# RWKV-6 attention and an MLP mixer on one core: the first batch's states, weight writes, loads and hand-written order

## The chip, the cores and the metric

The kernel runs on one core of a Trainium2 chip. The time is the device time of one launch in microseconds: 509.42 us is the median of three runs (509.24 to 509.84). One further execution was profiled; every duration below comes from that execution, whose span is 509.5 us.

## The reference

```python
B, H, S, D = 4, 8, 768, 48
state = zeros((B, H, D, D))
for t in range(S):                                   # attention, w lies in 0.8 to 0.95
    cur = einsum('bhd,bhe->bhde', u[None] * kt, vt)
    y[:, :, t] = einsum('bhd,bhde->bhe', rt, state + cur)
    state = wt[:, :, :, None] * state + einsum('bhd,bhe->bhde', kt, vt)
x = y.transpose(0, 2, 1, 3).reshape(B, S, H * D)     # 4 x 768 x 384
xt = x.transpose(0, 2, 1)                            # then the mixer
h = maximum(xt @ w_tok1, 0) @ w_tok2                 # 768 -> 256 -> 768 over tokens
u = x + h.transpose(0, 2, 1)
out = u + maximum(u @ w_ch1, 0) @ w_ch2              # 384 -> 1536 -> 384 over channels
```

The four mixer weights arrive as float64. The kernel loads their bits as pairs of 32-bit words and makes float32 of them on the chip.

## The kernel before, in words

**Units.** The attention of one batch is cut into three units of 256 tokens; `unit(i)` (from L352) makes the functions of unit i, called e0, e1, e2 for the first batch. A unit holds four chunks of 64 tokens (c = 0, 1 by j = 0, 1). Its steps, in order of need, are:
- `own_u` (ScalarE, four instructions, L278) multiplies the keys by u; `own_gram` (TensorE, L262) makes the products of a token with itself; `own_put` (VectorE, L400) masks them into `at`.
- `ends` (VectorE scan, L377) and `begins` (scan, L385) make the running products of w from both sides; `keys` (L382) and `queries` (L388) multiply k and r by them. `ranges` (ScalarE, L369) counts values outside a safe range; its result is read only near the end of the kernel.
- `tokens` (TensorE, eight transposes, L292) and `copied` (ScalarE, L293) turn the keys; `carry` (TensorE, `outer`, L308) makes each chunk's own part of the state, all four in one PSUM tile `kv_ps` that exists once.
- For each chunk, `scaled` (ScalarE, four instructions, L443, called t) multiplies the state by the chunk's whole decay into `before`, and `updates` (VectorE, L451 and L453, called s) adds the chunk's part from `kv_ps` into a new `state` in SBUF. This is a chain: t needs the s of the chunk in front of it, and s needs t.
- `gram` (L262) and `mask` (VectorE, L274) make the products of tokens within a chunk; `before()` (`across`, TensorE, L322), `seen` (ScalarE, L331) and `after` (`within`, TensorE, L343) form the output in PSUM, and `taken` (ScalarE, L349, three copies) moves it to `x`.

The grams and the outputs share two PSUM tiles (`ps_g`): each takes the tile that the second one before it gave back through its own_put, mask or taken.

**Weights.** `convert` (L202) works on a pair of blocks of 512 values per partition: `load` (two DMAs, L211), `exponent` (x, VectorE, L214), `raise_two` (p, ScalarE, L217), `mantissa` (m, VectorE, L220), `signs` (g, ScalarE, L223), `add` (VectorE, L226) and `put` (VectorE: one bf16 multiplication, L229, then one write for each block, L232). Three pairs hold w_tok1 and w_tok2 (`to_tok`, numbers 0 to 2), nine hold w_ch1 and w_ch2 (`to_ch`; its pair 0 is number 3 in the order below). The raw words lie in buffers, `bits64`; a load waits until the pair that used its buffer before is done.

**The prologue.** The first batch's three units, the `to_tok` conversions and the first mixer product `hidden` (h[2c + i], c a block of 128 tokens, i one of two halves, L747, two TensorE instructions each) stand in one order written out by hand: the call of `strict(...)` at the end of the planner's section. Each engine (TensorE, VectorE, ScalarE, and SP, which issues the DMAs) takes its own instructions in the order of that list. The relu of `hidden` (L749) closes the prologue, and `back` (L754) is the first TensorE work behind it. Loads called ahead of `strict` are issued first, in the order of the text: w0, rk0 (k then r), w1, v0, rk1, to_tok 0, rk2, v1, to_tok 1.

**After the prologue.** The mixer of batch b is interleaved with the attention of batch b + 1 by `interleaved`, a planner in the kernel that merges lists of pieces by due times (its costs are constants in the text). For the first batch these lists are the mixer, units 3 to 5, and `early_forms`: the `to_ch` conversions, three of the `ranges` (e1's second and e2's two; e1's first stands last in the hand-written list), and forms of the weights for the later batches. `back`, then the transposes to `xT` (L762, copied by ScalarE, L763) and `up` (L772) follow each other there.

**Buffers.** `ws` holds two buffers of w: units 0 and 2 share `ws[0]`, so w2 is loaded after unit 0's queries. `xpool` rotates two buffers of x; the first batch takes one of them.

## Time and profile before

| what | value |
| --- | --- |
| median of three runs | 509.42 us |
| span of the profiled execution | 509.5 us |
| mean granted TensorE clock | 0.981 of full |
| TensorE (PE) busy | 479.2 us, 94% of the span |
| weight loads of TensorE (PEld) busy | 404.4 us |
| VectorE (DVE) busy | 382.2 us |
| ScalarE (ACT) busy | 266.9 us |
| chain that ended last | PE 82%, DVE 8%, DMA 3%, ACT 3% |

Busy is the time in which an engine had an instruction in execution. A row of the timeline gives the start, the length, the engine, the line, the operation, the output and inputs, how many instructions are merged, and in brackets how long the engine stood idle ahead of it and what ended that wait. "issue" there means that the engine waited for nothing the profile shows. SPq is the queue of SP, from which nearly all DMAs are issued. The granted clock is the share of TensorE's full clock that the throttle let through.

### The profile page before, as it was taken

How to read it: one execution, taken by the hardware profiler on the slowest of the kernel's cores; microseconds unless marked ns; L12 is line 12 of the kernel's file. 1: busy time of each engine (PE TensorE's matmuls, PEld its weight loads, DVE VectorE, ACT ScalarE, POOL GpSimd, SP SyncE). 2: the span in 40 equal slices, each digit the busy share in tenths (PEclk: the TensorE clock that was granted, in tenths of full speed). 3: DMA queues.
4: the chain of work that ended last, by engine and by line, in shares of the span. 5: the costliest groups of instructions: out<-in, count | busy, mean ns of one | idle time of the engine just before them, and what ended most of it. 6: DMA issues, size and time to landing. Idle time of an engine off the chain costs nothing.

```text
span 509.5 us, 12748 instructions
## 1 busy us (share of the span) xinstructions
PE 479.2 (94%) x5218; PEld 404.4 (79%) x5218; DVE 382.2 (75%) x588; ACT 266.9 (52%) x631; POOL 53.2 (10%) x58
## 2 busy tenths in 40 slices
PE   3489999999999999999999999999999999999995
PEld 3477578866687667998989957999989958999995
DVE  7997998997764588787986948787985906566562
ACT  3876977755554544456545234556555324253350
POOL 0000000000000000311302000302212101130230
PEclk9769999999999999999999999999999999999999
DMA  8842937774560673583846571473725441345231
GB/s 305 321 177 64 302 115 257 243 220 136 158 196 26 192 216 116 177 233 99 262 122 210 187 249 60 140 227 97 258 70 156 143 153 48 98 135 171 78 111 50
DMA packets 48975, 83.76 MB, mean 164 GB/s; under 512 B 4816, under 2 KB 40272, under 8 KB 48912
## 3 DMA queue, kind: packets, MB, share of 16 engines
q1 hardware_dynamic: 48768, 82.90, 51.6%
q8 instruction: 42, 0.69, 0.6%
q14 instruction: 21, 0.17, 0.1%
q10 hardware_dynamic: 144, 0.00, 0.0%
HBM read 71.87 MB, written 11.01 MB: 163 GB/s over the span
## 4 chain that ended last, share of the span: by engine, by line
PE 82%; DVE 8%; DMA 3%; ACT 3%; issue 2%; SPq 0%; DVEq 0%; ACTq 0%
PE h_ps L783 9%; PE z_ps L772 9%; PE joint_ps L612 8%; PE ends_ps L641 7%; PE ends_ps L643 7%; PE o_ps L655 7%; PE o_ps L657 7%; PE o_ps L656 6%; PE h_ps L593 4%; PE h_ps L586 3%; PE gram L262 3%; PE kv_ps L308 3%; PE y_ps L343 2%; PE y_ps L322 2%; PE h_ps L747 2%
## 5 line engine op out<-in xcount | busy, mean ns | idle before, releaser
L634 POOL TENSOR_TENSOR z_high<-z_high 128x384 fp32r<-128x384 f32 x48 | 52.0, 1086 | 441.2 <-ACT z_high L619 237.6
L613 ACT ACTIVATE mid<-joint_ps 128x384 f32<-128x384 f32 x72 | 34.9, 485 | 64.5 <-PE joint_ps L612 63.3
L626 DVE TENSOR_TENSOR ends_ps<-ends_ps,mid 128x384 f32<-128x384 f32 x72 | 40.6, 563 | 32.4 <-PE ends_ps L643 19.8
L612 PE MATMUL joint_ps<-z_more,forms 128*128 128x384 f32 x216 | 51.6, 347 | 0.8 <-DVE z_more L564 0.8
L655 PE MATMUL o_ps<-forms,z_high 128*128 128x384 f32 x144 | 49.7, 345 | 1.7 <-DVE x L664 1.7
L641 PE MATMUL ends_ps<-x_forms,forms 128*128 128x384 f32 x216 | 49.5, 337 | 0.8 <-DVE z_high L630 0.8
L772 PE MATMUL z_ps<-xT,wch 128*128 128x256 f32 x216 | 49.4, 383 | 0.8 <-ACT xT L763 0.8
L643 PE MATMUL ends_ps<-x_forms,ring 128*128 128x384 f32 x216 | 49.3, 337 | 0.0
L657 PE MATMUL o_ps<-forms,z_high 128*128 128x384 f32 x144 | 48.8, 339 | 0.2
L783 PE MATMUL h_ps<-wch,z 128*128 128x384 f32 x144 | 48.5, 490 | 0.0
L656 PE MATMUL o_ps<-ring,z_high 128*128 128x384 f32 x144 | 48.5, 336 | 0.0
L443 ACT ACTIVATE before<-state,to_end 112x48 f32<-112x48 f32 x148 | 37.3, 326 | 19.1 <-DVE state L453 19.0
L772 PEld LDWEIGHTS z_ps<-xT,wch 128*128 128x128 f32 x216 | 40.1, 190 | 6.6 <-ACT xT L763 1.0
L783 PEld LDWEIGHTS h_ps<-wch,z 128*128 128x128 f32 x144 | 26.8, 190 | 17.1
L612 PEld LDWEIGHTS joint_ps<-z_more,forms 128*128 128x128 f32 x216 | 38.3, 188 | 2.4 <-DVE z_more L564 1.1
L664 DVE SCALAR_TENSOR_TENSOR x<-o_ps,x 128x384 f32<-128x384 f32 x36 | 19.8, 549 | 27.0 <-PE o_ps L656 26.8
L641 PEld LDWEIGHTS ends_ps<-x_forms,forms 128*128 128x128 f32 x216 | 38.6, 188 | 1.5 <-DVE z_high L630 1.5
L643 PEld LDWEIGHTS ends_ps<-x_forms,ring 128*128 128x128 f32 x216 | 38.5, 188 | 0.0
L655 PEld LDWEIGHTS o_ps<-forms,z_high 128*128 128x128 f32 x144 | 27.0, 188 | 2.9 <-DVE x L664 2.5
L657 PEld LDWEIGHTS o_ps<-forms,z_high 128*128 128x128 f32 x144 | 27.0, 188 | 1.5 <-DVE x L665 1.5
L622 ACT ACTIVATE z_high<-z_high 128x384 fp32r<-128x384 f32 x48 | 25.3, 526 | 4.1
L656 PEld LDWEIGHTS o_ps<-ring,z_high 128*128 128x128 f32 x144 | 27.1, 188 | 0.0
(153 smaller groups left out, 931.1 us busy)
## 6 DMA issues: line engine op xcount, KB each, us to landing
ring<-third SPq DMA_DIRECT2D x144, 192.0 KB, 3.6
raw<-in_w_ch_dram SPq DMA_DIRECT2D x16, 512.0 KB, 4.9
rk<-in_rk_dram SPq DMA_DIRECT2D x36, 192.0 KB, 5.5
near<-in_near_dram SPq DMA_DIRECT2D x8, 768.0 KB, 4.7
w<-in_w_dram SPq DMA_DIRECT2D x10, 520.5 KB, 3.7
vt<-in_v_dram SPq DMA_DIRECT2D x12, 384.0 KB, 3.5
out_dram<-x SPq DMA_DIRECT2D x18, 192.0 KB, 3.0
raw<-in_w_tok_dram SPq DMA_DIRECT2D x6, 512.0 KB, 9.5
```

The costliest lines, as they stand in the source:

```text
L443: act.mul(t[:ROWS, a], state[bt, g][:ROWS, a], by_last(c, j)[:, a:a + 1])
L612: pe.matmul(b, joint[m], xf[2][:, m], start=m == 0, stop=m == 2)
L613: act.mul(mid(jt), b, BASE / (BASE - 1.0))
L626: dve.tensor_add(a, a, mid(jt))
L634: pool.tensor_add(z_form(jt, 2), z_form(jt, 2).bitcast(f32), z_form(jt, 1).bitcast(f32))
L641: pe.matmul(a, up[m], xf[0][:, m], start=m == 0, stop=False)
L643: pe.matmul(a, low[:, m], xf[1][:, m], start=False, stop=m == 2)
L655: pe.matmul(a, z[0], up, start=first, stop=False, skip_group_check=True)
L656: pe.matmul(a, z[1], held[bt, s, half, 1, jt], start=False, stop=last, skip_group_check=True)
L657: pe.matmul(b, z[2], joint, start=first, stop=last, skip_group_check=True)
L772: pe.matmul(ps, now["wch1"][:, m, ts(jt, 128)], xT[:, m, ts(s, SEG)], start=(m == 0), stop=(m == DM // 128 - 1))
L783: pe.matmul(ps, zs[s][:, jt, ts(n, 128)], now["wch2"][:, jt, :], start=(jt == 0), stop=(jt == NJ - 1))
```

## The change

It has seven parts, all in the first batch or in the conversions:
- **States by TensorE.** For batch 0, `updates` makes no VectorE instruction any more. `outer` sets `start` only for the first product of each quarter and bank of `kv_ps`; `updates` multiplies `before` by the identity on TensorE (112 x 128 by 112 x 192, float32) and lets it accumulate onto the chunk's part in `kv_ps`. `scaled` then reads the state from PSUM.
- **Wider writes.** Where the two blocks of a pair lie so that one access pattern covers both, `put` writes them with one instruction of 1024 values; for pairs side by side the load lays the raw words out to match.
- **Constants.** Four copies and casts (L173, L174, L179) go from VectorE to ScalarE.
- **Places.** w2 gets the second x buffer, free in the first batch; `to_tok` 2 gets the buffer of `xT`, and each `to_tok` pair now has raw words of its own.
- **Loads first.** w2, rk2, all three `to_tok` pairs and `to_ch` 0 are issued ahead of the hand-written list.
- **Order.** The hand-written list is another one. It also holds the three `ranges` that were in the planner's list, and the relu is a step of its own, `rectified`.
- The planner's piece `ends` of unit 3 waits for one of the `ranges` no more.

```diff
@@ -123,8 +123,11 @@
 
+    second_x = xpool.tile([128, C, DM], f32, name="x")
+    ws.append(second_x.rearrange("p c e -> p (c e)")[:, :WCOLS])
+
     def w_of(i):
-        return ws[i % 2 if i <= UB else 1]
+        return ws[i if i < UB else 1]
 
@@ -170,13 +173,13 @@
     for j in range(2):
-        dve.tensor_copy(on_diagonal[ts(j, T)], ident[ts(j, T), ts(j, T)])
-    dve.tensor_copy(diagonal, on_diagonal)
+        act.copy(on_diagonal[ts(j, T)], ident[ts(j, T), ts(j, T)])
+    act.copy(diagonal, on_diagonal)
     pool.memset(strictly, 1.0)
...
                            pattern=[[1, T]], channel_multiplier=-1)
-    dve.tensor_copy(before_it, strictly)
+    act.copy(before_it, strictly)
 
@@ -206,9 +209,25 @@
 
+        (a, _), (b, _) = pair
+        c, k = a.shape[1:]
+        (row, _), (one, _) = a.ap[1:]
+        apart = b.offset - a.offset if a.tensor is b.tensor else None
+        beside = apart == k * one
+        if beside:
+            whole = bass.AP(a.tensor, a.offset, [list(a.ap[0]), [row, c], [one, 2 * k]])
+        elif apart is not None and (c == 1 or apart == c * row):
+            whole = bass.AP(a.tensor, a.offset, [list(a.ap[0]), [apart // c, 2 * c], [one, k]])
+        else:
+            whole = None
+
         def load():
             for n, (dst, src) in enumerate(pair):
-                sp.dma_start(d64[:, ts(n, 2 * PIECE)].rearrange("p (c k) -> p c k", c=dst.shape[1]), src)
+                if beside:
+                    to = d64.rearrange("p (c n k) -> p n c k", n=2, c=c)[:, n]
+                else:
+                    to = d64[:, ts(n, 2 * PIECE)].rearrange("p (c k) -> p c k", c=dst.shape[1])
+                sp.dma_start(to, src)
 
@@ -227,8 +246,8 @@
             dve.tensor_mul(factor, factor, sign)
-            for n, (dst, src) in enumerate(pair):
-                x, by = (t[:, ts(n, PIECE)].rearrange("p (c k) -> p c k", c=dst.shape[1]) for t in (mf, factor))
+            for dst, cols in [(whole, slice(0, 2 * PIECE))] if whole is not None else [(dst, ts(n, PIECE)) for n, (dst, _) in enumerate(pair)]:
+                x, by = (t[:, cols].rearrange("p (c k) -> p c k", c=dst.shape[1]) for t in (mf, factor))
                 dve.scalar_tensor_tensor(dst, x, 2.0 ** -20, by, op0=ALU.mult, op1=ALU.mult)
@@ -301,12 +320,14 @@
         kv = ps_a.tile([128, 2, 512], f32, name="kv_ps", tag="a")
+        begun = set()
         for c in range(UC):
...
                         pe.matmul(kv[ts(q, P), j, ds((c * A + a) * D, D)], kT[ts(j, T), c, a, ts(q, P)],
-                                  vt[ts(j, T), c, ts(2 * a + q, D)], start=True, stop=True)
+                                  vt[ts(j, T), c, ts(2 * a + q, D)], start=(q, j) not in begun, stop=True, skip_group_check=True)
+                        begun.add((q, j))
         return kv
@@ -444,7 +465,12 @@
             g = 2 * (half * UC + c) + j
-            if g < 2 * C - 1:
+            if g < 2 * C - 1 and bt == 0:
+                state[bt, g + 1] = L["kv"][:ROWS, j, ds(c * A * D, A * D)].rearrange("p (a e) -> p a e", a=A)
+                if g:
+                    pe.matmul(L["kv"][:, j, ds(c * A * D, A * D)], ident[:ROWS], L["before"][g][:ROWS].rearrange("p a e -> p (a e)"),
+                              start=False, stop=True, skip_group_check=True)
+            elif g < 2 * C - 1:
                 new = state[bt, g + 1] = apool.tile([128, A, D], f32, name="state", bufs=3)
@@ -745,8 +771,9 @@
             pe.matmul(sums[i], now["wtok1"][:, c, ts(i, 128)], x_of()[:, c, :], start=(c == 0), stop=(c == C - 1))
-            if c == C - 1:
-                act.activation(h1[:, i, :], sums.pop(i), AF.Relu)
+
+        def rectified(i):
+            act.activation(h1[:, i, :], sums.pop(i), AF.Relu)
 
@@ -787,7 +814,7 @@
 
-        return dict(hidden=hidden, back=back, turn=turn, up=up, down=down)
+        return dict(hidden=hidden, rectified=rectified, xT=xT, back=back, turn=turn, up=up, down=down)
 
@@ -811,7 +838,7 @@
         loads = piece(lambda: load_rk(i + 1), "loads")
-        ends = piece(e["ends"], "ends", ("DVE", 2.6, last("small", "large", "by3") + ((("of", 0),) if i == UB else ())))
+        ends = piece(e["ends"], "ends", ("DVE", 2.6, last("small", "large", "by3")))
         keys = piece(e["keys"], "keys", ("DVE", 1.25, k("ends")))
@@ -927,29 +954,35 @@
     h = [lambda i=i, c=c: turned["hidden"](i, c) for c in range(C) for i in range(DTOK // 128)]
-    to_tok = conversion((wtok1, w_tok1, 2, 256), (wtok2, w_tok2, 2, 256), rooms=lambda n: (n % 2, n % 2))
+    rectified = [lambda i=i: turned["rectified"](i) for i in range(DTOK // 128)]
+    bits64.append(turned["xT"].rearrange("p m t -> p (m t)").bitcast(u32)[:, :4 * PIECE])
+    to_tok = conversion((wtok1, w_tok1, 2, 256), (wtok2, w_tok2, 2, 256), rooms=lambda n: (3, 0) if n == 2 else (n, n))
     to_ch = conversion((now["wch1"], w_ch1, 1, 512), (now["wch2"], w_ch2, 4, 128), rooms=lambda n: (n % 2, 0, rks[2][:, ts(n % 2, PIECE)].bitcast(bf16)) if n else (2, 1))
+    load_w(2)
+    load_rk(2)
     to_tok[0][0]()
-    load_rk(2)
     load_v(1)
-    to_tok[1][0]()
+    for steps in (*to_tok[1:], to_ch[0]):
+        steps[0]()
 
     e0, e1, e2 = (unit(i) for i in range(UB))
-    (_, x0, m0, p0, add0, g0, put0), (_, x1, m1, p1, add1, g1, put1), (load2, x2, m2, p2, add2, g2, put2) = to_tok
-    load3, x3, m3, p3, add3, g3, _ = to_ch[0]
+    (_, x0, m0, p0, add0, g0, put0), (_, x1, m1, p1, add1, g1, put1), (_, x2, m2, p2, add2, g2, put2) = to_tok
+    _, x3, m3, p3, add3, g3, _ = to_ch[0]
     in_turn.update({pe.engine: None, dve.engine: None, act.engine: None, sp.engine: None})
     s0, s1, s2 = (e["updates"] for e in (e0, e1, e2))
     t0, t1, t2 = (e["scaled"] for e in (e0, e1, e2))
-    strict(*e0["own_u"], e0["ends"], e0["own_gram"], e0["begins"], e0["keys"], e0["tokens"], *e0["copied"], e0["queries"], lambda: load_w(2),
-           e0["gram"], *e1["own_u"], e1["ends"], e0["carry"], *e0["ranges"], e0["own_put"], e0["mask"], e1["own_gram"], s0[0], t0[1],
-           x0, p0, s0[1], t0[2], m0, g0, e1["begins"], s0[2], t0[3], add0, s0[3], t1[0], e0["before"], e0["seen"], put0, load2,
-           e1["keys"], e0["after"], *e2["own_u"], e1["tokens"], *e1["copied"], e1["queries"], e1["own_put"], e1["carry"], *e0["taken"],
-           lambda: load_v(2), e1["gram"], e2["ends"], g1, s1[0], t1[1], e2["keys"], e2["tokens"], s1[1], t1[2], e2["own_gram"], *e2["copied"],
-           e2["begins"], s1[2], t1[3], e1["mask"], load3, s1[3], t2[0], *h[:2], e2["carry"], e1["before"], h[2], e2["queries"], s2[0], t2[1],
-           e2["own_put"], e1["seen"], s2[1], t2[2], e2["gram"], x1, p1, e1["after"], m1, s2[2], t2[3], e2["mask"], h[3], add1,
-           e1["taken"][0], put1, to_ch[1][0], lambda: (load_w(3), load_rk(3), load_v(UB)), e2["before"], e2["seen"], *e1["taken"][1:],
-           x2, s2[3], e2["after"], *h[4:8], *e2["taken"], m2, p2, x3, add2, g2, m3, h[8], h[10], h[9], h[11], p3, put2, add3, g3,
-           to_ch[2][0], e1["ranges"][0])
+    strict(e0["ends"], e0["own_u"][0], e0["own_u"][1], e0["own_u"][2], e0["own_u"][3], e0["begins"], e0["own_gram"], e0["ranges"][0],
+           e0["ranges"][1], e1["own_u"][0], e0["keys"], e1["own_u"][1], e1["ends"], e0["queries"], e1["own_u"][2], e0["tokens"], e0["copied"][1],
+           e0["copied"][0], e1["own_u"][3], e0["own_put"], e1["ranges"][0], e1["begins"], e0["carry"], s0[0], e1["own_gram"], e1["keys"], t0[1],
+           s0[1], t0[2], e2["own_u"][0], e1["queries"], e2["own_u"][1], e0["gram"], e1["own_put"], x0, s0[2], e1["tokens"], t0[3], s0[3],
+           e2["own_u"][2], e1["copied"][0], t1[0], e1["copied"][1], lambda: load_w(3), p0, e0["before"], e0["mask"], e1["carry"], e0["seen"], g0,
+           e0["after"], s1[0], e2["own_u"][3], e0["taken"][0], t1[1], e2["own_gram"], e2["ends"], e0["taken"][1], s1[1], t1[2], m0, e0["taken"][2],
+           e2["keys"], e2["tokens"], lambda: load_rk(3), lambda: load_v(2), s1[2], e1["gram"], add0, x1, e2["copied"][0], t1[3], s1[3],
+           e2["own_put"], e2["copied"][1], to_ch[2][0], t2[0], e1["before"], put0, e2["carry"], e1["mask"], e2["ranges"][0], h[1], e1["seen"], s2[0],
+           e1["after"], e2["begins"], p1, m1, t2[1], g1, s2[1], e2["queries"], t2[2], h[0], add1, e2["gram"], e1["taken"][0], s2[2], h[2], x2,
+           e1["taken"][1], lambda: load_v(UB), e2["mask"], to_ch[1][0], t2[3], e1["taken"][2], m2, h[3], put1, e2["before"], p2, h[4], e2["seen"],
+           e2["after"], h[5], g2, h[6], add2, m3, h[7], g3, x3, e2["taken"][0], e2["taken"][1], e2["taken"][2], add3, h[8], h[9], p3,
+           e1["ranges"][1], put2, h[10], h[11], rectified[0], rectified[1], e2["ranges"][1])
 
@@ -1016,10 +1049,9 @@
         stored = [(("kept", i), lambda i=i: sp.dma_start(kept[i], (wtok1, wtok2)[i].rearrange("p c k -> p (c k)")), ()) for i in range(2)]
-        ranges = [(("of", n), f, (("ACT", 1.4, ()),)) for n, f in enumerate((e1["ranges"][1], *e2["ranges"]))]
         formed = [e for n in range(HALF) for e in splits(0, n)]
         late = [e for n in range(HALF) for e in splits(1, n)]
-        return first[:1] + each[1] + ranges + sum(each[2:], []) + stored + formed + late[:1] + late[5:6] + late[1:5] + late[6:-5 * AFTER], late[-5 * AFTER:]
+        return first[:1] + each[1] + sum(each[2:], []) + stored + formed + late[:1] + late[5:6] + late[1:5] + late[6:-5 * AFTER], late[-5 * AFTER:]
 
@@ -1115,6 +1147,7 @@
                 plain["hidden"](i, c)
+            plain["rectified"](i)
         for c in range(C):
```

## The prediction

> **What bounds the kernel now.** I first read the busy time of each engine by stretches (columns: stretch and length, then PE, PEld, DVE, ACT, POOL, granted clock, DMA share, GB/s).
>
> ```profile
> 0.00:54.00 54.00, 36.41 (x977) 28.77 (x977) 47.31 (x66) 34.91 (x89) 1.26 (x10) 0.84 0.63 224
> 54.00:70.00 16.00, 14.61 (x63) 9.81 (x64) 14.90 (x23) 15.20 (x26) 0.00 (x0) 1.00 0.82 237
> 70.00:100.00 30.00, 30.00 (x361) 25.86 (x360) 27.50 (x39) 21.94 (x49) 0.00 (x0) 1.00 0.64 204
> 100.00:140.00 40.00, 40.00 (x436) 25.71 (x435) 33.80 (x43) 22.70 (x47) 0.00 (x0) 1.00 0.58 180
> ```
>
> From 70 us on TensorE never stops, so whatever is saved there on another engine is worth nothing. In the first 54 us VectorE is the fullest engine and TensorE has 17.6 us of idle time, with a mean clock of 0.84. The change is worth what it does to the moment at which `back` (L754) starts, plus the 1.4 us that TensorE idles in 54 to 70. So I read the timelines of the first 56 us next, VectorE first, then TensorE, then SP.
>
> ```profile
> 16.93 0.34 DVE L451 COPY state<-kv_ps 112x192 f32<-112x192 f32 x1
> 18.35 0.35 DVE L453 TENSOR_TENSOR state<-before,kv_ps 112x192 f32<-112x192 f32 x1 [0.48 <-ACT before L443]
> 40.63 0.35 DVE L453 TENSOR_TENSOR state<-before,kv_ps 112x192 f32<-112x192 f32 x1 [2.70 <-PE kv_ps L308]
> 43.97 1.31 DVE L274 COPY_PREDICATED at<-before_it,gram 128x1024 f32<-128x1024 uint8 x1
> ```
>
> VectorE runs from 3.81 (first scan) nearly without a break; its two named stops stand at state updates, one behind e2's `carry`. The mask at 43.97 is e2's, the last VectorE work that e2's `after` needs.
>
> ```profile
> 18.39 0.85 PE L262 MATMUL gram<-rk,near 48*64 48x64 f32 x42 [1.94 <-issue]
> 32.68 1.58 PE L292 MATMUL k_ps<-ident,first 128*128 128x128 f32 x8 [1.73 <-issue]
> 36.11 2.93 PE L747 MATMUL h_ps<-x,wtok 128*128 128x384 f32 x4
> 46.91 1.15 PE L343 MATMUL y_ps<-vt,at 64*64 64x48 f32 x64 [0.27 <-ACT seen L331]
> 47.99 5.43 PE L747 MATMUL h_ps<-x,wtok 128*128 128x384 f32 x16
> 54.00 4.14 PE L754 MATMUL h_ps<-h,wtok 128*128 128x384 f32 x12 [0.58 <-ACT h L749]
> ```
>
> The end of the prologue is a tail: mask until 45.28, `after` until 48.06, eight `hidden` until 53.42, relu, `back` at 54.00: 8.7 us from the mask. Two stalls of 1.94 and 1.73 us are marked "issue". `hidden` costs 2.93/4 = 0.73 us an instruction at 36 us and 5.43/16 = 0.34 at 48 us: the granted clock is 0.50 to 0.53 in the stretches 20 to 30 and 35 to 40.
>
> **The change part by part.**
>
> *VectorE up to e2's mask.* I use the distance from one start to the next in an unbroken row, about 0.09 us under the printed length: scan with memset and reciprocal 2.55 (2.80 for e0's), begins 2.25, keys and queries 1.13, own_put 1.12, mask 1.20, exponent and mantissa 0.60, add 1.13, put 0.72 + 1.21. The new list puts these ahead of e2's mask or ends with it: three ends 7.90, three begins 6.75, six keys and queries 6.78, three own_put 3.36, three masks 3.60, x0, m0, x1, m1, x2 3.00, two adds 2.26, put0 1.86 (0.72 and one wide write; the nearest row of 128x1024 float32 from SBUF, L226, is 1.22 long against 1.29 for two halves, so 0.07 less). Sum 35.5; 3.81 + 35.5 = 39.3. The same count for the old list adds 11 updates at 0.26 (2.9), the four constants (10.02 to 10.64, 0.62) and 0.07, and lacks add1 and x2 (1.73), which it had behind the mask: 37.4, to 41.2. The mask really left VectorE at 45.2, so 4.0 us were waits: 2.70, 0.48 and small ones. By VectorE alone the mask comes 5.9 us earlier, if no wait is left.
>
> *The order's tail.* From mask to `back` the new order has `after`, seven `hidden` (h5 to h11; the last four behind `taken`) and the relus: three `taken` 1.45 and the last four `hidden` 2.7, with `after` 1.2, `before`'s rest 1.3 and the relu 0.6, plus 0.6 in which ScalarE still finishes g3 ahead of `taken` and 0.7 of hand-overs. That is 8.6, the same. ScalarE has p3 (1.14) and e1's second ranges (1.34) between `taken` and the relu, 2.5 beside 2.7 of `hidden`: just hidden; a late p3 would delay the relu by as much. put2 is the last VectorE work: 39.3 + m2 0.60, put1 1.93, add2 1.13, m3 and x3 1.20, add3 1.13, put2 1.86 = 47.2, and `back` needs it only from its third block, 2.7 us in.
>
> *States on TensorE.* An add has no row. Its two passes over 192 columns are bounded below by 2 x 0.12 (L292, 128 columns, x8 in 0.97 at full clock) and above by 2 x 0.34 (L747, 384 columns); by columns 0.34, with some 0.16 to drain. Ten of them: 3.4 us of TensorE, 2.4 to 6.8. As a link of the chain an add takes about 0.5 where the VectorE add took 0.35; a link is then 0.5 + 1.01 (L443, four instructions) + two hand-overs of 0.07, 1.65 against 1.5. Eleven links are 18 us, spread over some 24, so the chain binds only where TensorE is late. TensorE takes its list in order: while an add waits for ScalarE, the next gram or transposes behind it wait too, and their mask or copy. e1's `carry` now also waits until t of e1's first chunk has read `kv_ps`.
>
> *TensorE's own sum* up to e2's `after`: per unit own_gram 1.08, tokens 0.95, carry 1.05, gram 1.08, before 1.1, after 1.1 = 6.4, three times 19.1; adds 3.4; five `hidden` 3.4: 25.9 us at full clock, from 8.4 on (rk0 lands at 8.1 at the latest) to 42.4: 34.0, so 8.1 of slack. The two first steps ran at half clock in the old trace too (1.98 and 1.94): 1.9. If the "issue" stalls come again: 3.7. A small product at half clock takes about 1.7 times as long (1.96 against 1.15 for L343), so a cold microsecond loses 0.41. With both charges 2.5 us are left, enough for 6 us of cold clock; before it was 17 us.
>
> *The clock.* In the old trace it fell at about 19.5, after a stretch with 1.6 us of work in 3.4, and at 33.1, after one with 1.7, and came back at 29.7 and 40. The new list keeps TensorE at 25.9/34 = 76% of the time, against 21.8/39.7 = 55%, so I expect less cold time, some 7 us. [...]
>
> *Placed one by one.* I put each instruction at the later of its engine's previous one and its inputs. The old list, with the old cold stretches, so gives e2's `after` at 48.2 (48.06 in the trace) and `back` at 54.2 (54.00). The new one gives 48.5 warm without stalls, 50.3 warm with both stalls, 50.3 with 10 cold microseconds without, 51.7 with 7 cold and both stalls. I take **50.3**, 3.7 us earlier.
>
> *Loads.* SP has eight DMAs in flight (v1 was issued at 9.38, when w1 landed). At the old rate, 390 to 404 GB/s from 10 to 20 us, the new sequence lands w2 at 14, rk2 at 16.6, to_tok 0 at 19.3 (was 15.3; needed at 20.4), v1 at 20.2, to_tok 1 and 2 at 22.9 and 25.6, to_ch 0 at 28.2, and behind w3 and rk3 v2 at 32.6, where e2's `carry` wants it at 31.7 to 34: at most 0.9 us, counted in the placing. In the old list SP stood from 13.4 to 23 for put0's buffer.
>
> *The mixer after 54.* ScalarE sheds three or four ranges of 1.34 between 55.9 and 65.5, where it is at 15.2 of 16 and TensorE waits for `xT` copies; of the 1.4 us idle there, 0.6 is the relu. I take 0.4 of the remaining 0.8, bounds 0 and 0.8. The constants on ScalarE (under 1 us) lie in its 3.9 us wait for rk0. The other wide puts, seven at 0.07, and `ends` freed from its ranges lie beside a saturated TensorE: 0.
>
> Sum: 3.7 + 0.4 = 4.1 off the span of 509.5, 505.4; the median of the runs shown stands 0.1 below that span: **505.3 us**.
>
> **The rivals.**
> - *VectorE's sum decides.* TensorE keeps up, warm and without stalls: `back` at 48.5, 5.5 earlier, and 0.8 in the mixer: 503.2 on the span, 503.1 on the median. For it: 76% use. Against it: the stalls lay where DMA was busy, and the new list keeps it full until 32.
> - *TensorE becomes the bound* and it gets slower: with both stalls and ten or more cold microseconds behind the start, its adds, taken in order, pass each delay on to the next gram and its mask. Ten cold ones place `back` at 54.5, the old 17 at 56.2: 0.5 to 2.2 later, 509.9 to 511.6. It decides from 9 cold microseconds on with both stalls. For it: the first steps start cold and e0's gram no longer follows straight on the transposes. Against it: fuller stretches.
> - *Given back in the mixer.* `interleaved` gets other lists and so another merge; VectorE is at 92% from 70 to 100, and where its conversions came late for `up`, TensorE would wait what it gained. VectorE's list ends 6 us earlier too, which speaks against it. A loss of 3.7 gives 509.0.
>
> **How the numbers follow.** Forecast 0.50, VectorE's sum 0.27, given back 0.10, TensorE bound 0.13. The range runs from 502.6 (48.5, all of the mixer's idle, 0.5 for adds at their lower bound) to 509.4 (`back` level with before), leaving out some 0.05 below and 0.12 above. A difference of 0.2% (1.0 us) is what can be told from no change here: faster than 508.4 has 0.80, within 0.10, slower than 510.4 0.10.
>
> **What would show it.** `back`'s first row at 50.3, e2's mask at 41 to 43; no L451 or L453 on VectorE before `back`; ten more TensorE rows of 112x192 in the state's line; the 2.70 stop gone; fewer than 10 cold microseconds; v2 landing by 33; TensorE idle under 1 us in the 16 us behind `back`. I am wrong if TensorE's rows wait on ScalarE's `before` for more than 6 us in all, if the clock stays at 0.5 past 30, or if `back` comes early and the end does not follow.

## The result and the profile after

The changed kernel takes 516.57 us (median of four executions, 514.80 to 516.58) against 509.36 before: a ratio of 1.0126, 95% interval 1.0106 to 1.0146. It is slower, outside the predicted range. The ratios below leave out one slow execution, of `al_warm_vec` (689.24 us at a mean clock of 0.653).

The profiled execution has a span of 513.1 us against 509.5, so 3.6 us of the loss are in the traces. The other half is not: in every execution the time is 1.7 us above the span, but the traced execution of before (511.19 us, left out of the median) was 1.8 above its median, and that of after (514.80) 1.8 below. The untraced ones left a span and a mean clock (514.8 to 514.9 us at 0.986 to 0.991, against 513.1 at 0.981), no more.

Where the 3.6 us lie, by the view of busy time by stretches (stretch, length, PE, PEld, DVE, ACT, POOL, granted clock, DMA share, GB/s):

```profile
0.00:54.00 54.00, 37.92 (x989) 30.91 (x989) 42.54 (x47) 35.94 (x96) 1.26 (x10) 0.84 0.80 273
70.00:100.00 30.00, 29.00 (x312) 25.04 (x313) 27.02 (x34) 21.53 (x47) 0.00 (x0) 1.00 0.59 192
...
24.00:27.00 3.00, 3.00 (x84) 2.54 (x86) 2.97 (x3) 2.40 (x8) 0.00 (x0) 0.71 1.04 400
27.00:30.00 3.00, 2.85 (x127) 2.39 (x127) 0.70 (x2) 3.00 (x7) 0.00 (x0) 1.00 1.06 347
30.00:33.00 3.00, 0.07 (x3) 0.00 (x0) 2.40 (x3) 1.01 (x4) 0.00 (x0) 0.93 1.04 229
33.00:36.00 3.00, 2.27 (x47) 2.07 (x47) 0.68 (x1) 0.00 (x0) 0.00 (x0) 0.50 1.03 328
```

VectorE shed 4.8 us (47.31 to 42.54), as meant, and TensorE's mean clock is the 0.84 of before. DMA share rose from 0.63 to 0.80. From 30 to 33 TensorE works 0.07 of 3 us, with the DMA full; from 33 to 36 the others follow. TensorE's timeline (start, length, engine, line, operation, output and inputs, count, and in brackets the wait ahead and its end) names that hole:

```profile
16.66 1.01 PE L471 MATMUL kv_ps<-before,ident 112*128 112x192 f32 x2
20.54 1.55 PE L281 MATMUL gram<-rk 48*64 48x64 f32 x45 [2.04 <-issue]
33.73 1.55 PE L281 MATMUL gram<-first,near 48*64 48x64 f32 x45 [3.65 <-issue]
44.84 0.59 PE L471 MATMUL kv_ps<-before,ident 112*128 112x192 f32 x2
50.84 1.15 PE L364 MATMUL y_ps<-vt,at 64*64 64x48 f32 x64
57.33 4.14 PE L781 MATMUL h_ps<-h,wtok 128*128 128x384 f32 x12 [0.58 <-ACT h L776]
71.00 1.13 PE L799 MATMUL z_ps<-xT,wch 128*128 128x256 f32 x4 [1.71 <-DVE wch L251]
```

The gram of 64 instructions breaks after its 19th, and TensorE stands 3.65 us on nothing that the profile shows. `back` starts at 57.33 instead of 54.00, 3.3 later; behind it the span has 455.8 us, before 455.5. The loads that fill the DMA up to 36 us are not only the ones that the change puts first: the new order also issues w3 at 20.84 and rk3 at 22.17, which before issued at 48.38 and 48.86 (rk3 in after, then in before):

```profile
22.17 5.27 SPq L144 DMA_DIRECT2D rk<-in_rk_dram  x4
```

```profile
48.86 2.17 SPq L141 DMA_DIRECT2D rk<-in_rk_dram  x4
```

VectorE, no longer the fullest engine, hands the hole on in the second and third of these waits (the first, for ScalarE, stands ahead of the hole, and TensorE comes to the transposes of these keys only at 36.00):

```profile
29.43 1.23 DVE L403 TENSOR_TENSOR first<-first 112x1024 f32<-112x1024 f32 x1 [2.30 <-ACT near L297]
35.32 1.23 DVE L421 TENSOR_TENSOR at<-gram,u_rows 128x1024 f32<-128x1024 f32 x1 [2.93 <-PE gram L281]
40.11 1.31 DVE L293 COPY_PREDICATED first<-before_it,gram 128x1024 f32<-128x1024 uint8 x1 [1.70 <-PE gram L281]
47.24 1.31 DVE L293 COPY_PREDICATED at<-before_it,gram 128x1024 f32<-128x1024 uint8 x1 [0.16 <-PE gram L281]
```

**What "issue" is here.** Counting TensorE's instructions from its first, the two waits stand in front of the 222nd and the 476th. In the kernels below such waits come behind instruction 221, 348, 475, 602, 730, 858 and 986 (some one off), every 127 or 128, whatever the work is there. One other place occurs, in the old order alone: ahead of e2's transposes, where TensorE waits for `keys`. The page of the profile lists the DMA queues; one of them has, with packets, MB and share,

```profile
q8 instruction: 43, 0.70, 0.6%
```

that is 16 KB at a time, 43 times, for 5238 TensorE instructions: one for each 122, close to the 127 or 128 between the waits. The author's reading of these counts: TensorE's program itself comes in blocks by this queue, and an "issue" wait is TensorE at the end of a block with the next not there. The blocks' starts, in us, from the trace's DMA records:

```
                 1st   2nd   3rd   4th   5th   6th   7th
before          15.9  22.3  27.4  31.5  38.0  43.5  47.0
after           18.0  24.3  30.8  36.7  40.7  44.6  49.8
a_late_w3_rk3   18.1  24.4  28.0  32.1  38.2  41.8  47.5
b_traffic       16.2  22.5  27.9  37.3  44.7  48.8  54.8
al_warm         14.2  20.4  26.6  33.0  37.0  40.7  46.6
al_paced        14.7  20.2  23.8  28.8  32.5  38.0  43.9
```

The transfer itself takes 0.9 to 1.6 us in every row. What differs is the distance: in after 5.9 to 6.5 us while the DMA share is above 1, up to 36, and then 4.0 and 3.8. (Where TensorE waits for no block, the distance is also how slowly it uses them: 6.5 in before from 31.5 on, with a DMA share of 0.01. And a high share alone does not fix it: in before the 4th came 4.1 behind the 3rd, at shares of 0.95 and then 0.53.) Each wait ends 2.2 to 3.1 us behind the start of the block of its number: in after at 20.54 (1st, 18.0) and 33.73 (3rd, 30.8). In before the 3rd starts at 27.4 and TensorE gets there later: no wait. That the pace of the blocks hangs on other loads is what these rows suggest; the experiments test it.

### The profile page after: what moved, and what is told of

It is laid out like the page before. It is cut to its first block, busy times and chain, and to the rows that moved or that the text cites. A ratio compares the mean times of both kernels' runs of the same rounds, so it can differ in the third digit from the quotient of the medians.

```text
span 513.1 us, 12764 instructions
## 1 busy us (share of the span) xinstructions
PE 483.4 (94%) x5238; PEld 407.9 (79%) x5238; DVE 378.2 (74%) x564; ACT 265.9 (52%) x635; POOL 53.2 (10%) x58
## 4 chain that ended last, share of the span: by engine, by line
PE 75%; DVE 10%; DMA 9%; ACT 3%; issue 2%; SPq 1%; DVEq 0%; ACTq 0%
PE z_ps L799 9%; PE joint_ps L638 8%; PE ends_ps L667 7%; PE ends_ps L669 7%; PE o_ps L681 7%; PE o_ps L683 7%; PE o_ps L682 6%; PE h_ps L619 4%; PE h_ps L810 4%; PE h_ps L612 3%; PE gram L281 3%; PE y_ps L343 2%; DMA third<-ring 2%; DMA raw<-in_w_tok_dram 2%; PE kv_ps L328 2%
## 5 line engine op out<-in xcount | busy, mean ns | idle before, releaser
L810 PEld LDWEIGHTS h_ps<-wch,z 128*128 128x128 f32 x144 | 26.8, 190 | 17.1
L464 ACT ACTIVATE before<-state,to_end 112x48 f32<-112x48 f32 x132 | 33.2, 325 | 12.4 <-DVE state L479 12.4
```

Of the source, the lines that this page charges most:

```text
L464: act.mul(t[:ROWS, a], state[bt, g][:ROWS, a], by_last(c, j)[:, a:a + 1])
L810: pe.matmul(ps, zs[s][:, jt, ts(n, 128)], now["wch2"][:, jt, :], start=(jt == 0), stop=(jt == NJ - 1))
```

## The experiments

The theories. **FETCH**: the loads issued earlier than before (those put first, and w3 and rk3) fill the DMA engines, TensorE's program arrives late, and the loss is that. **ADDS**: the additions on TensorE, in order behind ScalarE, hold the grams back. **CLOCK** (COLD in two expectations): half clock makes TensorE the bound. **ORDER**: the new places of the steps make the waits. Ratios are to the kernel before on the same chip, with 95% intervals.

### The additions or the loads

**a_vec_adds**, the additions back on VectorE:

```diff
-            if g < 2 * C - 1 and bt == 0:
...
-            elif g < 2 * C - 1:
+            if g < 2 * C - 1:
```

> The changed kernel with the first batch's state additions back on VectorE, all else as changed. Theory ADDS (the ten additions take 6.4 us of TensorE's list, start to next start, and TensorE is now the bound): back starts 4 to 6 us earlier, at 51 to 53, and the median falls to 510 to 512. Theory FETCH (the two waits marked issue, 2.04 and 3.65 us, are what was lost): they stay, at the 221st and about the 475th plus the adds left out of the count, and back stays at 56 to 57.5. Theory ORDER (the new places of the steps make the waits): back stays within 1 us of 57.3.

517.72 us, 1.0157 (1.0128 to 1.0186), `back` at 59.82, later than any of the theories had it. The wait at 475 grew:

```profile
35.53 1.34 PE L281 MATMUL gram<-first,near 48*64 48x64 f32 x37 [6.19 <-issue]
```

ADDS alone cannot explain the loss; with the same loads it is there without them.

**a_late_loads**, four loads later (the pairs `to_tok` 2 and `to_ch` 0, w3 and rk3):

```diff
-    for steps in (*to_tok[1:], to_ch[0]):
-        steps[0]()
+    to_tok[1][0]()
...
-           e2["own_u"][2], ..., lambda: load_w(3), p0,
+           e2["own_u"][2], ..., p0,
...
-           lambda: load_rk(3), lambda: load_v(2), s1[2],
+           lambda: load_v(2), s1[2],
...
-           e2["own_put"], ..., to_ch[2][0], t2[0],
+           e2["own_put"], ..., to_ch[2][0], to_tok[2][0], to_ch[0][0], lambda: load_w(3), lambda: load_rk(3), t2[0],
```

> The changed kernel with the loads of the third w_tok pair, of w_ch's first pair, of w3 and rk3 moved behind v2 and w_ch's third pair, so that few bytes are in flight from 24 to 31 us. FETCH with contention: the issue wait of 3.65 us at about 30 us shrinks to 2 or less, back comes 1.5 to 3 us earlier (54.5 to 56), median 513 to 515. ADDS or ORDER: the wait may shrink but TensorE's list stays as long; back moves by less than 1 us.

516.55, 1.0141 (1.0114 to 1.0168), `back` at 58.06. No time is won: by the time this is what was expected of ADDS or ORDER, and FETCH's 513 to 515 was missed. And yet no wait is left at 475, where the DMA share is now 0.02 (24 to 27 us) and 0.16 (27 to 30). New ones of 1.59, 1.50 and 2.76 us stand at 730, 858 and 986 (39.94, 46.69 and 53.99 us), where the share is 0.97 to 1.06; each ends 2.5 to 2.7 us behind the start of a block (37.5, 44.0, 51.3). The wait went where the loads went.

**b_pe_adds**, the kernel before with nothing but the additions on TensorE (the hunks of `outer` and `updates` in the change's diff):

> The kernel before with the first batch's state additions on TensorE alone, its order and loads kept. ADDS: TensorE's list grows by 5 to 7 us while VectorE loses 2.9, so the time rises, to 511 to 514. FETCH or ORDER: TensorE had 17 us of idle time in the old order, VectorE's relief shows, 506.5 to 509.

515.03, 1.0100 (1.0072 to 1.0129), `back` at 58.16. In the old order ADDS is right: the additions wait in TensorE's list for ScalarE (four of them, 3.3 us in all; two are shown), and what is behind them waits too. VectorE, for its part, waits 7.32 us for e2's gram ahead of its last mask.

```profile
22.10 1.01 PE L452 MATMUL kv_ps<-before,ident 112*128 112x192 f32 x2 [0.97 <-ACT before L445]
38.36 1.01 PE L452 MATMUL kv_ps<-before,ident 112*128 112x192 f32 x2 [1.10 <-ACT before L445]
```

In after no addition has such a bracket.

**a_shift**, 16 more small TensorE instructions ahead of everything, whose result is unused:

```diff
+    early_bank = bank("early")
+    for _ in range(8):
+        pe.matmul(early_bank[:, :T], ident, ident[:, :T], start=True, stop=True)
```

> The changed kernel with eight more small float32 products on TensorE early (16 records), nothing else changed. If the issue waits are instruction fetches they stay tied to the count of TensorE's records: the first stands again at the 221st record, that is 16 products earlier in the list, and not at the same product. If they are tied to a product's own wait, they stay at the same product, the 20th of the second gram. Time: within 1 us of the changed kernel.

515.57, 1.0117 (1.0091 to 1.0143). At 221 no wait stands now: TensorE comes there at 21.87, 4.4 us behind the start of that block, against the expectation. The other wait is again behind instruction 475, now 16 instructions earlier in the work: the same gram breaks after its 3rd instruction instead of its 19th.

```profile
34.84 1.98 PE L281 MATMUL gram<-first,near 48*64 48x64 f32 x61 [5.16 <-issue]
```

The place hangs on the count, not on any data, which of the theories only FETCH explains.

### Parts one by one

**a_late_w3_rk3**, after with only the loads of the second batch (w3, rk3, v3) at the end of the hand-written list:

```diff
-           e2["own_u"][2], ..., lambda: load_w(3), p0,
+           e2["own_u"][2], ..., p0,
...
-           lambda: load_rk(3), lambda: load_v(2), s1[2],
+           lambda: load_v(2), s1[2],
...
-           e1["taken"][1], lambda: load_v(UB), e2["mask"],
+           e1["taken"][1], e2["mask"],
...
-           rectified[0], rectified[1], e2["ranges"][1])
+           rectified[0], rectified[1], lambda: load_w(3), lambda: load_rk(3), lambda: load_v(UB), e2["ranges"][1])
```

> The changed kernel with only w3, rk3 and v3 loaded at the end of the hand-written list. FETCH with contention: the fetch that follows the 348th record no longer meets rk3's packets, and the wait at the 475th record falls from 3.65 to 2 us or less, with no new wait ahead of the 858th; back at 55 to 56. If contention has no part in the wait, it stays at 3 to 6 us at the 475th record. A later collision is possible behind back, where w3 and rk3 now land, so the median may move less: 513.5 to 516.

510.12 (ten executions, 509.09 to 512.42), 1.0014 (0.9999 to 1.0029): 0.9 above before on the same chip (509.20), so that 6.3 us of the 7.2 lost are gone, more than FETCH had expected (513.5 to 516), with no instruction of TensorE, VectorE or ScalarE touched. The traced execution is the slowest of the ten. By stretches, to set beside the same rows of after:

```profile
27.00:30.00 3.00, 2.86 (x128) 2.45 (x128) 0.71 (x2) 3.00 (x7) 0.00 (x0) 1.00 0.21 78
30.00:33.00 3.00, 2.82 (x64) 2.30 (x58) 3.00 (x4) 2.35 (x10) 0.00 (x0) 1.00 0.51 147
```

With a DMA share of 0.21 the 3rd block starts at 28.0, 2.8 us earlier than in after, and the 4th at 32.1, 4.7 earlier; TensorE works through, and the clock, which in after falls at 32.6 within the wait, stays full. Its timeline keeps the wait at 221, has a new one at 730, which was not expected, and `back` at 54.09:

```profile
20.61 1.55 PE L281 MATMUL gram<-rk 48*64 48x64 f32 x45 [2.02 <-issue]
40.64 0.92 PE L364 MATMUL y_ps<-vt,first 64*64 64x48 f32 x48 [1.66 <-issue]
```

**b_loads_first**, before with the change's places and loads first, in the old order (their later calls are taken out of the list):

```diff
+    second_x = xpool.tile([128, C, DM], f32, name="x")
+    ws.append(second_x.rearrange("p c e -> p (c e)")[:, :WCOLS])
...
+    load_w(2)
...
-    to_tok[1][0]()
+    for steps in (*to_tok[1:], to_ch[0]):
+        steps[0]()
...
```

> The kernel before with the change's places and its loads issued first, in the old order (w3, rk3 and v3 where they were, additions on VectorE). FETCH with contention: DMA is full until 28 us without a break, so the waits marked issue up to the 475th record grow by 1 to 4 us in sum, and as VectorE waits for the gram behind them the kernel is 1 to 3 us slower than before, 510.5 to 512.5. If early loads are harmless: 508.5 to 510.

511.45, 1.0037 (1.0024 to 1.0050), `back` at 55.23: this part alone makes it slower. The time is the one that was expected, but the reason is another. The waits at 221 and ahead of e2's transposes are 1.89 and 1.33 us, no longer than before's 1.94 and 1.73, and none stands at 475. What is new is that `to_tok` 0, now behind w2 and rk2, lands later than the old order asks for it, and the states behind it wait too:

```profile
21.01 0.69 DVE L217 TENSOR_SCALAR raw<-raw 128x1024 uint16<-128x1024 uint16 x1 [3.60 <-DMA raw<-in_w_tok_dram]
```

So this run does not speak for FETCH; in after the same step waits for nothing that the view shows.

**b_wide_consts**, before with the wider writes and the constants on ScalarE (those hunks of the change's diff):

> The kernel before with the wider writes and the constants on ScalarE alone. By VectorE's sum 0.62 + 0.14 us come off the prologue: 508.5 to 509.2. If VectorE's relief is eaten by the waits for TensorE: 509.2 to 510.

509.03, 0.9989 (0.9973 to 1.0005): nothing that can be measured.

**a_old_order**, after with the old hand-written list and planner's lists, all else of the change:

> All of the change but its order: additions on TensorE, wider writes, constants, places and loads first, with the order, the ranges and the relu of before. If the order is what costs (ORDER), this is faster than the changed kernel by 3 us or more, 513 or less. If the additions and the fetches cost whatever the order: 514.5 to 518, with back at 57 to 60.

515.13, 1.0101 (1.0071 to 1.0131), `back` at 58.99. ORDER by itself, by which this had to be 513 or less, is not the cause. Nor is it FETCH here: the only "issue" wait is the one at 221 (2.22), while VectorE waits 4.47 us for `to_tok` 0's data and an addition 3.08 for ScalarE. The losses of b_pe_adds (1.0%) and b_loads_first (0.4%) sum to 1.4%; the intervals are too wide to tell that from the 1.0% here.

### Additions and clock, with the loads out of the way

**al_vec_adds**, a_late_w3_rk3 with the additions on VectorE (the diff of a_vec_adds):

> The changed kernel with w3, rk3 and v3 loaded late, and the additions back on VectorE. ADDS: with the fetch at the 475th record out of the way, TensorE's list is 6 us shorter, back comes 3 to 5 us earlier than with the additions on TensorE (54.1 there), 49 to 51, and the median is 505 to 507. If VectorE's list is as full with them as TensorE's was: 509 to 511, with waits of VectorE for ScalarE's before of 2 us and more.

514.02, 1.0080 (1.0055 to 1.0104), 3.9 us behind a_late_w3_rk3, where ADDS had expected 505 to 507. VectorE now waits at its additions:

```profile
23.36 0.35 DVE L474 TENSOR_TENSOR state<-before,kv_ps 112x192 f32<-112x192 f32 x1 [1.08 <-ACT before L464]
28.29 0.35 DVE L474 TENSOR_TENSOR state<-before,kv_ps 112x192 f32<-112x192 f32 x1 [3.36 <-ACT near L297]
```

TensorE also has "issue" waits of 2.11, 1.46 and 2.08, 5.7 in all against 3.7; how much of the 3.9 us is VectorE's own was not separated. So in the new order the additions belong on TensorE, in the old one on VectorE; ADDS as the cause of after's loss has fallen.

**al_warm**, a_late_w3_rk3 with nine TensorE products of ones ahead of the first steps, to bring the clock up, results unused:

```diff
+    def fill(n, cols):
+        for _ in range(n):
+            pe.matmul(filled[:, 0, :cols], ident, filler[:, :cols], start=True, stop=True)
...
-    strict(e0["ends"], e0["own_u"][0],
+    strict(lambda: fill(7, 256), e0["ends"], e0["own_u"][0],
...
-           e0["tokens"], e0["copied"][1],
+           e0["tokens"], lambda: fill(2, 512), e0["copied"][1],
```

> The changed kernel with w3, rk3 and v3 loaded late and nine filler products on TensorE, seven ahead of the first gram and two behind the first transposes, which keep it at work from 2 to 8 and in the wait at 12 to 14 us; their results are used by nothing. COLD (10 us at half clock from 15.5 on cost 4 us of TensorE's list, the first 4 us another 1.9): granted clock 1.0 from 9 us to 20 at least, back at 49.5 to 52, median 505.5 to 508.5. If the clock does not matter, because ScalarE and VectorE are as late: 509.5 to 510.5.

511.45, 1.0036 (1.0023 to 1.0048), `back` at 54.72, slower than either expectation. The clock was full from 6.7 to 30.6, where a_late_w3_rk3 has it half from 15.6 to 25.8, and it bought nothing:

```profile
29.27 1.16 PE L281 MATMUL gram<-first,near 48*64 48x64 f32 x63 [3.53 <-issue]
```

TensorE came to the block's end earlier and waited there. CLOCK is not the bound while the blocks are.

**b_warm**, b_wide_consts with the first seven of these products:

> The kernel before with the wider writes, the constants on ScalarE and seven filler products ahead of the first gram. In the old order VectorE sets the pace and TensorE falls cold again at 19.5: within 0.5 us of the same kernel without fillers, 508.5 to 509.5. If the early clock carries: 507 or less.

508.81, 0.9985 (0.9967 to 1.0003). `back` is at 52.51, 1.5 earlier than before, but the time can't be told from no change.

**al_warm_vec**, al_warm and al_vec_adds together:

> Both together: w3, rk3 and v3 late, additions on VectorE, filler products. ADDS and COLD: 503.5 to 506.5, VectorE's sum the bound, back at 48.5 to 51. If VectorE's own waits for ScalarE's before bound it: 507 to 510.

512.55, 1.0058 (1.0040 to 1.0077), `back` at 56.28: slower than both expectations, and not to be told from al_vec_adds.

### The traffic alone, and a version that beats both

**b_traffic**, before with ten copies of 512 KB of unused data from memory to memory, issued behind the load at 27 us:

```diff
+    spill = [dram.tile([128, COLS], f32, name=f"spill{i}") for i in range(10)]
...
-           e1["mask"], load3, s1[3],
+           e1["mask"], load3, *[lambda i=i: sp.dma_start(spill[i], rk[3 + i // 2, i % 2]) for i in range(10)], s1[3],
```

> The kernel before with ten copies of 512 KB from HBM to HBM issued behind the load at 27 us, of data that nothing uses, so that the DMA engines have work from 28 us to past 40, where they stood idle. FETCH with contention: the fetches at 31.5, 38.0 and 43.5 move to 6 us and more apart, TensorE waits at the 602nd, 730th and 857th record (issue), and back comes 3 us or more later: median 512 to 517. If full queues do not slow the fetches, the order and the results of the step are as before: 509 to 510, back at 54.

516.30, 1.0123 (1.0084 to 1.0162), `back` at 60.64: no engine got work, and 6.8 us are lost, about as much as in after. Two rows of before, then the same of b_traffic, by stretches:

```profile
33.00:36.00 3.00, 3.00 (x71) 2.66 (x69) 3.00 (x3) 2.48 (x9) 0.00 (x0) 0.51 0.01 3
36.00:40.00 4.00, 4.00 (x48) 2.21 (x42) 1.94 (x3) 1.42 (x6) 0.00 (x0) 0.51 0.01 4
```

```profile
33.00:36.00 3.00, 3.00 (x76) 2.29 (x74) 3.00 (x3) 2.48 (x9) 0.00 (x0) 1.00 1.05 393
36.00:40.00 4.00, 0.84 (x16) 0.32 (x14) 2.02 (x3) 1.50 (x7) 0.00 (x0) 1.00 0.97 326
```

The DMA share goes from 0.01 to 1 and TensorE from 4.00 busy to 0.84, although its clock is now full. Its waits in b_traffic, behind instructions 602 and 729:

```profile
40.05 0.84 PE L308 MATMUL kv_ps<-vt,kT 64*64 64x48 f32 x31 [2.67 <-issue]
47.72 1.23 PE L262 MATMUL gram<-first 48*64 48x64 f32 x35 [3.15 <-issue]
```

No wait of TensorE, VectorE or ScalarE from 20 to 62 us names a load there, so that it is not data that came late. FETCH's mechanism is shown by itself.

**al_paced**, al_warm with four conversion loads later, three of them each behind a tiny DMA that reads the result of a VectorE step, the fourth (`to_ch` 2) behind `put1`; x1 also moves, behind e2's `begins`:

```diff
+    def pace(t):
+        n = len(paced)
+        paced.append(dram.tile([1, 16], f32, name=f"paced{n}"))
+        sp.dma_start(paced[n], t)
...
+           lambda: pace(to_ends[0][0:1, :16]), to_tok[1][0], e0["taken"][1],
...
+           e1["mask"], lambda: pace(ats[1][0:1, 0, 0, :16]), to_tok[2][0], e2["ranges"][0],
...
+           e2["queries"], lambda: pace(rks[2][0:1, :16]), to_ch[0][0], t2[2],
...
+           put1, to_ch[2][0], e2["before"],
```

> The changed order with additions on TensorE, filler products as in al_warm, w3, rk3 and v3 late, and the second and third w_tok pairs, w_ch's first and its third each held back behind a step of VectorE by a copy of 64 bytes, so that the DMA engines pause between 20 and 50 us; x1 stands behind e2's begins. FETCH with contention: fetches after 20 us 3.4 to 4.5 us apart, the wait of 3.53 us at the 475th record gone, back at 50.5 to 52.5 (54.7 in al_warm), median 506 to 508.5. If the waits were not from the loads: back at 54 to 56, 510 to 512.

508.90, 1.0006 (0.9978 to 1.0035): level with before, `back` at 51.85, 5.5 ahead of after. The wait at 475 shrank to 0.79, but the later `up` waits for a weight that its conversion brings too late:

```profile
26.36 1.16 PE L281 MATMUL gram<-first,near 48*64 48x64 f32 x63 [0.79 <-issue]
65.52 1.13 PE L799 MATMUL z_ps<-xT,wch 128*128 128x256 f32 x4 [1.71 <-DVE wch L251]
```

**al_paced2** puts five steps of that conversion at the end of the hand-written list:

```diff
-           rectified[0], rectified[1], lambda: load_w(3),
+           rectified[0], rectified[1], to_ch[1][1], to_ch[1][3], to_ch[1][2], to_ch[1][4], to_ch[1][5], lambda: load_w(3),
...
+        each[1] = [piece for piece in each[1] if piece[0][2] in ("put", "load")]
```

> al_paced with all but the last step of w_ch's second pair done at the end of the hand-written list, in VectorE's idle time behind the prologue, in place of the planner's list. If the mixer gave the gain back through that pair's late write: the wait of 1.71 us at the first up falls under 0.8, the median comes 1 to 2 us under al_paced, 506.8 to 508. If TensorE only waits elsewhere for as long: 508.5 to 509.5.

507.10 (eleven executions), 0.9961 (0.9939 to 0.9982): faster than before by 0.4%, and than after. The wait for `wch` is gone and `back` is at 52.76, although the wait at 986 is longer than al_paced's 0.64:

```profile
47.02 0.44 PE L364 MATMUL y_ps<-vt,at 64*64 64x48 f32 x14 [1.46 <-issue]
```

## Why the prediction was wrong

The direction was wrong. The rival that came nearest is "TensorE becomes the bound": its stalls and its 17 cold microseconds came, the delays of its additions did not, and the time lies above its 509.9 to 511.6. The step that failed is the price of the "issue" stalls in TensorE's own sum, together with the loads, for which only the landing of their data was priced.

- **VectorE's sum: near, and without weight.** L451 and L453 are gone. By VectorE alone e2's mask was to end at 39.3; it ended at 48.55. Of the 44.6 us up to there 8.2 are waits, so the work is 36.5 against 35.5 forecast. The tail, 8.6 predicted, took 8.8 (48.55 to 57.33).
- **TensorE's own sum: it failed in three terms.** *"If the 'issue' stalls come again: 3.7"* took two waits of before for a fixed charge. The second of them (1.73 at 32.68) was none: TensorE waited there for `keys`, which ended at 32.58, and no block ended there:

```profile
31.37 1.21 DVE L382 TENSOR_TENSOR first<-first 112x1024 f32<-112x1024 f32 x1
```

  The real waits of after are 2.04 + 3.65 = 5.7. The prediction had the sign in hand ("the stalls lay where DMA was busy, and the new list keeps it full until 32") and kept the old price. *The clock*: 7 cold microseconds forecast; it was half from 15.5 to 25.7 and 32.6 to 39.4, 17.1 us, as much as before (and so "past 30", one of the prediction's signs of being wrong). The second stretch starts in the fetch wait and is absent from a_late_w3_rk3, so it hangs on the wait; the first is there in both. *The additions*: from one start to the next ten took 6.4 us against 3.4, about 0.47 at full clock and 0.78 to 0.94 at half; within the bounds of 2.4 to 6.8, near the upper one. Put into the prediction's sum, from 8.26: 25.9 + 1.9 for the first two steps (1.98 and 1.92 long, as before's gram of 1.99 at 34.19 and its transposes of 1.97 at 26.34, where the granted clock was 0.5; the trace's clock records begin at 12.07) + 5.7 of fetch + (17.1 - 3.2 that lie in waits) x 0.41 = 5.7 of cold + 1.3 for the additions at full clock + 2.05 of named waits (1.90 for ScalarE's `kT`, 0.15) end e2's `after` at 50.8; it ended at 52.0, and 1.2 us stay without a name.
- **Loads: priced by landing alone.** "At most 0.9 us" asked when each load's data come. v2 landed at 36.26 instead of 32.6 and held nothing up only because TensorE came to e2's `carry` as late as 41.52: that part was luck. What a full DMA does to the pace of the blocks (5.9 to 6.5 us apart in after, up to 36) was in no term. This is the cause of the loss: a_late_w3_rk3 moves three loads and regains 6.3 of 7.2 us, b_traffic adds only traffic and loses 6.8.
- **States on TensorE: "each delay passed on" right as a mechanism, elsewhere.** The brackets behind `before` came in the old order (b_pe_adds), not in after, which waited for blocks instead; with the loads paced the new order has one too (1.10 at 37.92 in al_paced2). `scaled` from PSUM, costed as from SBUF at 1.01 for four, took 0.87.
- **The mixer: -0.4 forecast, +0.3 measured.** The ranges are off ScalarE there, but `up` now waits 1.71 for `wch`, where before it waited 0.76 for `xT`: "given back in the mixer" came true in small.
- **Constants and wider writes: nothing that can be measured** (b_wide_consts, 0.9989), as the mixer's 0 for them had it; the 0.7 us that they take off VectorE ahead of the mask did not show.

Open: why the untraced executions of after are 1.8 us longer than the traced one; that a_late_w3_rk3 regains most of the whole 7.2 speaks for later blocks there too, but no trace shows it. What holds a block's start back under traffic, when its transfer takes no longer, and how far ahead of its use it is asked for, was not measured. So the runs show that the traffic delays the blocks, not by what law. Fewer TensorE instructions in the prologue, which would need fewer blocks, was not tried.

## What to carry to other kernels

A load issued early was not free here where it landed in time: with the DMA share above 1, TensorE of after got a block, 127 or 128 instructions, per 5.9 to 6.5 us, and small instructions used them up faster than that (128 between 27 and 30 us of a_late_w3_rk3). Count the instructions in front of an "issue" wait; where the counts of several lie one fixed number apart (here 127 or 128), thin out the traffic that is not needed yet (here the next batch's loads) before touching any engine's work. Landing in time is a question of its own: the same early loads cost 0.4% in the old order by bringing one that was needed sooner too late (b_loads_first). An edit that helped in one order (the additions on TensorE, 3.9 us in the new one with w3, rk3 and v3 late) cost in another (1.0% in the old one, b_pe_adds), so a part's worth holds only beside the bound it was measured with.

## What the runs showed of the hardware

- Blocks of 16 KB on the queue `q8 instruction`, read here as TensorE's program, came every 5.9 to 6.5 us with the DMA share above 1, and 4.0 us apart with it at 0.2 (after, ahead of and behind 36 us), though each took only 0.9 to 1.3 us to move. In b_traffic the 3rd and 4th are 9.4 us apart.
- A clock regained early was worth nothing in al_warm: it runs warm from 6.7 to 30.6 us, and its wait at 475 is 3.53 where the kernel without it has none.
- The clock of after fell at 15.5 and at 32.6. In the 3.4 us ahead of the first TensorE had worked 1.5 us, with a wait of 1.90 as the longest gap; in the 3.4 us ahead of the second 0.9 us, and it had then stood still for 2.5 us. Since the first product no gap ahead of either was longer than these 2.5. In before the clock fell at 19.4 and 33.1, and the longest gap between its first product and 33.1 was 2.12.
- ScalarE's four scalings of 112x48 took 0.86 to 0.92 us from PSUM (after) and 0.99 to 1.01 from SBUF (before).
